# Seven staging tiles instead of four for the weight loads of an expert layer, in a pool that closes before the next layer's pool opens

## The chip, the core and the metric

The kernel runs on one core of a Trainium2 chip. The core has a matrix engine (TensorE, "PE" in the rows, with its weight loads as "PEld"), a vector engine (VectorE, "DVE"), a scalar engine (ScalarE, "ACT"), GpSimd ("POOL"), and SyncE ("SP"), whose queue issues most of the DMA transfers. Each engine works through its own instruction stream in program order, and an instruction that waits holds up everything behind it on that engine. The metric is the time of one execution in microseconds; lower is better.

## What is computed

The reference chains three layers over 1,536 tokens of width 512, all in float32:

```
attn = clustered attention over q, k, v     # 2 batches, 8 heads, 768 positions, 64 wide
x    = attn as [1536, 512]
# first expert layer: 8 experts, each token goes to one of them
e    = argmax(x @ w_gate)
y[t] = gate_w[t] * eom[t, e] * (relu(x[t] @ w1[e]) @ w2[e])   # w1 [8,512,1024], w2 [8,1024,512]
# second layer, dense
h    = y @ w_in                       # [512, 2048]
out  = (h * sigmoid(h)) @ w_out       # [2048, 512]
```

## The kernel before, in words

After the attention, `moe1` runs the first expert layer and `moe2` the dense second layer. The instruction order of each engine comes from the framework's scheduler, which orders the instructions by a simulated timeline; the kernel's own calls set what may run and from which buffers.

**Weights.** Each float32 weight block of 128 partitions by 1,024 numbers (512 KB) is loaded by one DMA of the SP queue into a staging tile (line 925), and then split into a high and a low part, which fill one half each of a tile `w` of the pool `wp` (16 tiles, two experts' worth). ScalarE writes the high part (line 894), and VectorE or GpSimd subtracts it from the staging tile to get the low part (line 899; with the `wn` counter every third one goes to GpSimd). The staging tile comes free when that subtraction has ended. The first twelve blocks stage in `wp` itself; from then on `stage()` takes tiles of tag `raw` from the pool `gp`, four of them. The queue holds loads in program order, so a load that waits for a staging tile also holds back the loads behind it and the reads of token rows (line 828).

**Units.** The first layer is a list of ten units: experts 1 to 5 with two blocks of 128 tokens each, one single-block unit for overflowing tokens, experts 6 and 7, and the two blocks of expert 0 as single-block units. Each unit needs eight weight blocks. A unit `expert(...)` runs eight groups of twelve matmuls (`hp`, line 1000); after each group ScalarE takes the Relu (`HH`, line 1001) and VectorE its low part (`HL`, line 1002); then come the matmuls of the second product (`yp`, line 1016, with `HH` and `HL` as stationary operands), the scaling `ys` (line 1021) and an indirect DMA of GpSimd that scatters the rows to `x2` (line 818). Between the groups the unit calls the next weight loads, eight per unit. Single-block units go through a transposed form (`hr`, `htp`, `H`, lines 981 to 988) and take one staging tile for `hr`. The labels tile `f` of a unit (lines 944 and 945) takes one of three buffers, which the scatter of an earlier unit still reads.

**Second layer.** The weights `w_in` and `w_out` arrive as 64-bit numbers, 32 loads of 512 KB ("halves" below). Each goes through two ScalarE operations and two VectorE operations on the staging tile (lines 1166 to 1171), then the same split, the low part always on GpSimd. The first four blocks (eight halves of `w_in`) are called from `moe1`, the other 24 halves from `moe2`, one block per step f of its first token block (`w2.pop(0)()`). `load2` reads the token rows back from `x2` (line 828), transposes them (`tp`, line 1201) and splits them into `XH` and `XL`. Steps f=0 to 15 then multiply by `w_in` (`hp`, line 1246), take the sigmoid (lines 1252 and 1253), split into `GH` and `GL`, and multiply by `w_out` (`op`, line 1225); `sg`, `GH` and `GL` are two tiles each in `gp`.

So `gp` holds four staging tiles of 4 KB a partition and six tiles of 2 KB, 28 KB a partition. It opens when `free()` closes the pools of the attention's rows, and lives to the end.

Of the kernel before, what the change touches and what calls it, by code (L numbers as in the profile page):

```python
# [11 lines left out]
F32 = mybir.dt.float32  # L12
# [18 lines left out]
class Att:  # L31

    def __init__(s, tc, ctx, q, k, v, cent, const, ident, xb, router=None):
        s.tc = tc
        s.nc = tc.nc
        s.q_ = q
        s.k = k
        s.v = v
        s.cent = cent
        s.xb = xb  # L40
        s.router = router
        P = lambda name, bufs, **kw: ctx.enter_context(tc.tile_pool(name=name, bufs=bufs, **kw))
        s.const = const
        s.ident = ident
        s.ld = P('att_ld', 2)
        s.ns = P('att_ns', 1)
        s.ohp = P('att_oh', 1)
        s.mkp = P('att_mk', 1)
        s.qk = P('att_qk', 2)
        s.cp = P('att_c', 1)  # L50
        s.sm = P('att_sm', 3)
        s.sm2 = P('att_sm2', 2)
        s.pp = P('att_pp', 4)
        s.p16 = P('att_p16', 3)
        s.pt = P('att_pt', 4)
        s.vp = P('att_v', 2)
        s.vq = P('att_vq', 1)
        s.ps_s = P('ps_s', 2, space=PSUM)
        s.ps_t = P('ps_t', 3, space=PSUM)
        s.ps_o = P('ps_o', 1, space=PSUM)  # L60
# [570 lines left out]
class Moe:  # L631

    def __init__(s, tc, ctx, const, ident, wg, wog, w1, w2, w_in, w_out, out, xb):
        s.sc = {}
        s.wn = 0
        s.gp = None
        s.spare = None
        s.hold0 = 1
        s.lows = []
        s.tc = tc  # L640
        s.nc = tc.nc
        s.c = const
        s.ident = ident
        s.w1 = w1
        s.w2 = w2
        s.w_in = w_in
        s.w_out = w_out
        s.out = out
        s.xb = xb
        s.wg = wg  # L650
        s.wog = wog
        dr = ctx.enter_context(tc.tile_pool(name='dram', bufs=1, space=bass.MemoryType.DRAM))
        s.xo = dr.tile([NCH * 128, RW], F32, name='xo')
        s.xst = dr.tile([E * CAP, RW], F32, name='xst')
        s.x2 = dr.tile([2 * NT * 128, DM], F32, name='x2')
# [253 lines left out]
    def stage(s):  # L909

        if s.gp:
            return s.gp.tile([128, 1024], F32, tag='raw', name='stage', bufs=4)
        if s.spare is None:
            t = s.wp.tile([128, 2, 1024], F32, tag='w', name='stage2')
            s.spare = t[:, 1]
            return t[:, 0]
        t = s.spare
        s.spare = None
        return t
# [347 lines left out]
def build(tc, q, k, v, centroids, moe_w_gate, moe_w_output_gate, moe_w1, moe_w2, moe2_w_in, moe2_w_out, out):  # L1267
    nc = tc.nc
    with ExitStack() as ctx:
        const = ctx.enter_context(tc.tile_pool(name='const', bufs=1))  # L1270
        ident = const.tile([128, 128], F32, name='ident')
        make_identity(nc, ident)
        cx = ExitStack()
        xp = cx.enter_context(tc.tile_pool(name='xbp', bufs=1, side='right'))
        xb = [xp.tile([128, NT, RW], F32, name=f'xb{b}') for b in range(2)]
        m = Moe(tc, ctx, const, ident, moe_w_gate, moe_w_output_gate, moe_w1, moe_w2, moe2_w_in, moe2_w_out, out, xb)
        with ExitStack() as c3:
            m.consts(cx.enter_context(tc.tile_pool(name='route', bufs=1, side='right')))
            att = Att(tc, c3, q, k, v, centroids, const, ident, xb, router=m.pair)
            att.ones = m.ones  # L1280
            m.att = att
            att.bgdma = [lambda d=d, z=z: nc.sync.dma_start(d, z) for d, z in m.zeros()]
            att.after_load = m.load_router
            att.run()
        m.pools(ctx)

        def free():
            cx.close()
            return ctx.enter_context(tc.tile_pool(name='gp', bufs=2, side='right', reuse_waits='tile'))
        X, w2 = m.moe1(m.weights2(), free)  # L1290
        with tc.high_priority():
            m.chunks = nc.values_load(m.tot[0:1, 0:1], min_val=1, max_val=NCH, skip_runtime_bounds_check_because='chunk count is bounded by the token count')
        m.moe2(m.gp, X, w2)
        m.rest()
# [18 lines left out]
```

## Time and profile before

| what | value |
|---|---|
| median of 3 runs | 793.61 us (791.09 to 793.64) |
| profiled execution, its own time | 794.19 us |
| span of the trace in that execution | 792.5 us |
| PE busy over the span | 742.1 us, 94% |
| loads of `w1` and `w2` | 72 of 512 KB each |
| loads of `w_in` and `w_out` | 32 of 512 KB each |

The profiled execution is 0.58 us above the median; 1.7 us of it lie outside the span. Times in rows are microseconds from the span's start. The first expert layer runs from about 280 to 497 us, the second layer from there to the end; attention comes before.

### The profile page before, as it was taken

To read this page: it belongs to the slowest core of one execution; us is meant where nothing else is said; L and a number is where in the kernel's file an instruction comes from. 1 tells how busy PE (TensorE), PEld (TensorE's weight loads), DVE (VectorE), ACT (ScalarE), POOL (GpSimd) and SP (SyncE) were. 2 spreads that over 40 slices of the span, in tenths; PEclk is the share of its full clock that TensorE was granted. 3 is DMA by queue.
4 is the path that set the end of the run, shared out by engine and by line. 5 is a ranking of instruction groups with operands and counts; after the bars stand their busy time and mean duration, and the time that the engine had idled before them with its cause. 6 is when DMAs were issued, how large, how long until landed. Compare 5 with 4: busy or idle time off the path is not lost.

```text
span 792.5 us, 14080 instructions
## 1 busy us (share of the span) xinstructions
PE 742.1 (94%) x5498; PEld 625.6 (79%) x5498; DVE 467.7 (59%) x830; ACT 433.7 (55%) x703; POOL 318.1 (40%) x259
## 2 busy tenths in 40 slices
PE   7889999999997799999999999799999999999996
PEld 6788998999887478888978877587687888878885
DVE  6769887977785565555557683789524222232222
ACT  5769889988764435654556663788423222122222
POOL 5677878788631365443334552445300000000000
PEclk8779999999988899999999999999999999999999
DMA  8879998998993377876658735756101000010001
GB/s 270 173 151 215 200 181 176 188 195 179 196 171 121 137 259 229 296 268 230 205 159 285 261 116 191 242 166 207 34 1 53 1 1 0 1 54 0 1 1 55
DMA packets 132983, 116.30 MB, mean 147 GB/s; under 512 B 97607, under 2 KB 103751, under 8 KB 132912
## 3 DMA queue, kind: packets, MB, share of 16 engines
q1 hardware_dynamic: 129632, 109.03, 52.0%
q0 software_dynamic: 3280, 6.33, 2.1%
q8 instruction: 44, 0.72, 0.4%
q14 instruction: 27, 0.22, 0.1%
HBM read 71.67 MB, written 18.45 MB: 114 GB/s over the span
## 4 chain that ended last, share of the span: by engine, by line
PE 53%; DVE 14%; issue 11%; DMA 10%; ACT 6%; POOL 5%; POOLq 0%; ACTq 0%; DVEq 0%; SPq 0%
PE op L1225 14%; PE hp L1246 13%; DMA stage<-in_moe_w 4%; PE yp L1016 4%; PE sp L398 3%; PE hp L1000 3%; POOL w L899 3%; PE sp L400 3%; DVE m L419 3%; DMA x<-ys,f 3%; DVE pt L456 2%; PE tp L190 2%; ACT p L421 2%; PE ptp L445 2%; DMA stage<-in_moe_w_out 2%
## 5 line engine op out<-in xcount | busy, mean ns | idle before, releaser
L899 POOL TENSOR_TENSOR w<-stage,w 128x512 fp32r<-128x512 f32 (+1 forms) x54 | 101.3, 1880 | 120.5 <-ACT w L894 113.8
L1246 PE MATMUL hp<-XH,w 128*128 128x512 f32 (+1 forms) x392 | 124.3, 394 | 3.9 <-DVE sg L1253 3.1
L894 ACT ACTIVATE w<-stage 128x1024 fp32r<-128x1024 f32 (+1 forms) x104 | 96.6, 942 | 55.0 <-DMA stage<-in_moe_w 30.2
L419 DVE TENSOR_REDUCE m<-sp 128x1 f32<-128x768 f32 x96 | 91.2, 952 | 38.8 <-PE sp L400 34.0
L1225 PE MATMUL op<-w,GH 128*128 128x512 f32 x384 | 113.2, 397 | 0.0
L465 POOL TENSOR_TENSOR p<-p,p 128x768 f16<-128x768 f32 x58 | 95.2, 1650 | 38.3 <-DVE p L464 27.8
L1253 DVE TENSOR_TENSOR sg<-hp,sg 128x512 f32<-128x512 f32 (+1 forms) x49 | 33.3, 679 | 118.2 <-ACT sg L1252 118.2
L421 ACT ACTIVATE p<-sp,m 128x768 f32<-128x768 f32 x96 | 86.3, 899 | 16.1 <-DVE m L419 15.4
L1000 PEld LDWEIGHTS hp<-X,w 128*128 128x128 f32 x672 | 86.1, 188 | 11.0 <-DVE HL L1002 5.8
L1000 PE MATMUL hp<-X,w 128*128 128x256 f32 x672 | 89.8, 283 | 4.0 <-DVE HL L1002 3.1
L1252 ACT ACTIVATE sg<-hp 128x512 f32<-128x512 f32 (+1 forms) x49 | 28.8, 589 | 116.8 <-PE hp L1246 115.8
L1246 PEld LDWEIGHTS hp<-XH,w 128*128 128x128 f32 x392 | 73.2, 188 | 23.0 <-DVE sg L1253 4.8
L1225 PEld LDWEIGHTS op<-w,GH 128*128 128x128 f32 x384 | 71.9, 188 | 17.5 <-ACT GH L894 0.7
L899 DVE TENSOR_TENSOR w<-stage,w 128x1024 fp32r<-128x1024 f32 x50 | 67.9, 1371 | 28.9 <-ACT w L894 27.3
L1246 PE MATMUL hp<-XL,w 128*128 128x512 f32 (+1 forms) x196 | 75.1, 391 | 1.6 <-DVE XL L899 1.6
L1225 PE MATMUL op<-w,GL 128*128 128x512 f32 x192 | 68.3, 397 | 1.3 <-DVE GL L899 1.3
L1016 PE MATMUL yp<-w,HH 128*128 128x512 f32 x224 | 63.7, 401 | 3.0 <-ACT HH L1001 2.7
L489 PE MATMUL o<-vh,pt 128*128 128x66 f16 x576 | 64.6, 198 | 0.4 <-DVE pt L456 0.4
L491 PE MATMUL o<-vh,pt 128*128 128x66 f16 x576 | 63.5, 195 | 1.5 <-issue 1.5
L398 PE MATMUL sp<-KA,QA 128*128 128x384 f32 x192 | 61.0, 400 | 3.2 <-ACT p L421 2.7
L490 PE MATMUL o<-vl,pt 128*128 128x64 f16 x576 | 63.9, 194 | 0.2 <-issue 0.2
L489 PEld LDWEIGHTS <-pt 128*128 128x128 f16 x576 | 53.6, 99 | 9.7 <-issue 8.6
(216 smaller groups left out, 1432.3 us busy)
## 6 DMA issues: line engine op xcount, KB each, us to landing
stage<-in_moe_w SPq DMA_DIRECT2D x72, 512.0 KB
stage<-in_moe_w_in SPq DMA_DIRECT2D x16, 512.0 KB
stage<-in_moe_w_out SPq DMA_DIRECT2D x16, 512.0 KB
xst<-z SPq DMA_DIRECT2D x8, 516.0 KB
xt<-xst SPq DMA_DIRECT2D x6, 516.0 KB
vt<-in_v SPq DMA_DIRECT2D x4, 768.0 KB
xt<-x SPq DMA_DIRECT2D x6, 512.0 KB
out_x<-os SPq DMA_DIRECT2D x12, 256.0 KB
```

What stands on the lines that cost most here:

```text
L398: nc.tensor.matmul(sp[:, g, :384], lhsT=QA[:, t], rhs=KAf[:, g * 384:(g + 1) * 384], start=True, stop=False)
L419: st['min'] = nc.vector.tensor_reduce(m, sv, axis=AX.XY, op=ALU.min).ins
L421: st['exp'] = nc.scalar.activation(p32, sv, AF.Exp, bias=m, scale=-1.0).ins
L465: s.nc.gpsimd.tensor_sub(p16[:, 1], p32, p16[:, 0])
L489: nc.tensor.matmul(o[:, t, 0:D + 2], lhsT=pt[:, 0, kt], rhs=vh[:, kt], start=kt == 0, stop=False)
L490: nc.tensor.matmul(o[:, t, 0:D], lhsT=pt[:, 0, kt], rhs=vl[:, kt], start=False, stop=False)
L894: s.nc.scalar.activation(hi, src, AF.Copy)
L899: f = lambda: (eng or s.nc.vector).tensor_sub(lo, src, hi).ins
L1000: nc.tensor.matmul(hp, lhsT=W1[k][w][:, f * 128:(f + 1) * 128], rhs=x[:, k, :N], start=n == 0, stop=n == 11)
L1016: nc.tensor.matmul(yp, lhsT=h[:, f, i * 128:(i + 1) * 128], rhs=w, start=n == 0, stop=n == 23)
L1225: nc.tensor.matmul(op[i], lhsT=g[:, i * 128:(i + 1) * 128], rhs=w, start=f == 0 and m == 0, stop=f == 15 and m == 2)
L1246: nc.tensor.matmul(h, lhsT=I[k, f // 8][w][:, fs], rhs=x[:, k, c], start=n == 0, stop=n == 11)
```

## The change

Two staging pools take the place of one. `free()` now opens a pool `wst` that holds only staging tiles, seven of them (28 KB a partition, what `gp` took as a whole). It is closed after `moe1` has been written out, and `gp` with its four staging tiles and its six tiles for the second layer is opened on the same space; a tile of `gp` then waits until the tiles of `wst` under it have been released.

```diff
@@ -634,6 +634,7 @@
         s.gp = None
+        s.raws = 7
         s.spare = None
@@ -909,7 +910,7 @@
         if s.gp:
-            return s.gp.tile([128, 1024], F32, tag='raw', name='stage', bufs=4)
+            return s.gp.tile([128, 1024], F32, tag='raw', name='stage', bufs=s.raws)
@@ -1286,8 +1287,12 @@
         def free():
             cx.close()
-            return ctx.enter_context(tc.tile_pool(name='gp', bufs=2, side='right', reuse_waits='tile'))
+            return cy.enter_context(tc.tile_pool(name='wst', bufs=2, side='right', reuse_waits='tile'))
+        cy = ExitStack()
         X, w2 = m.moe1(m.weights2(), free)
+        cy.close()
+        m.raws = 4
+        m.gp = ctx.enter_context(tc.tile_pool(name='gp', bufs=2, side='right', reuse_waits='tile'))
```

The scheduler then orders some instructions anew (lines of the changed kernel are one higher from 637 on). Three places matter below.

On the SP queue, at the end of the first layer (`w_in` and `w_out` are loads of second-layer halves, `xt_7251` and `xt_7267` are the first reads of `x2`). Before:

```order
L925 DMA stage<-in_moe_w 128x1024 x4
L925 DMA stage<-in_moe_w 128x2x512 x4
L1161 DMA stage<-in_moe_w_in 128x1024 x8
L1161 DMA stage<-in_moe_w_out 128x1024 x2
L828 DMA xt_7251<-x_72 128x2x512
L828 DMA xt_7267<-x_72 128x2x512
L1161 DMA stage<-in_moe_w_out 128x1024 x5
```

and in the changed kernel:

```order
L1162 DMA stage<-in_moe_w_in 128x1024 x8
L829 DMA xt_7251<-x_72 128x2x512
L829 DMA xt_7267<-x_72 128x2x512
L1162 DMA stage<-in_moe_w_out 128x1024 x6
L829 DMA xt_7770<-x_72 128x2x512
```

The first two loads of `w_out` moved behind the reads of `x2`, because their staging tiles now belong to `gp`.

On ACT, around the last single-block unit (`hr` and `H`) and the first `XH` of the second layer. Before:

```order
L984 ACTIVATE stage<-hr 128x512 x2
L1166 ACTIVATE stage<-stage 128x512
L1169 ACTIVATE stage<-stage 128x512
L894 ACTIVATE H<-htp 128x512 x2
L1166 ACTIVATE stage<-stage 128x512
L1169 ACTIVATE stage<-stage 128x512
L894 ACTIVATE w<-stage 128x512 x2
L1166 ACTIVATE stage<-stage 128x512
L1169 ACTIVATE stage<-stage 128x512
L894 ACTIVATE XH<-tp_7253 128x4x128
L894 ACTIVATE XH<-tp_7260 128x4x128
```

and in the changed kernel:

```order
L985 ACTIVATE stage<-hr 128x512 x2
L895 ACTIVATE H<-htp 128x512 x2
L895 ACTIVATE XH<-tp_7253 128x4x128
L1167 ACTIVATE stage<-stage 128x512
L1170 ACTIVATE stage<-stage 128x512
L1167 ACTIVATE stage<-stage 128x512
L1170 ACTIVATE stage<-stage 128x512
L895 ACTIVATE XH<-tp_7260 128x4x128
```

The work on the first halves of `w_out` moved from ahead of `H` to behind the first `XH`.

On DVE, in expert 3's unit (`f` is the labels tile, `w_5782` and `w_5802` are low parts of weight blocks). Before:

```order
L899 TENSOR_TENSOR w_5782<-stage,w_5782 128x1024
L944 COPY f<-xt 128x2 x2
L945 COPY f<-xt 128x2
L899 TENSOR_TENSOR w_5802<-stage,w_5802 128x1024
L1002 SCALAR_TENSOR_TENSOR HL<-hp,HH 128x256 x3
```

and in the changed kernel:

```order
L900 TENSOR_TENSOR w_5782<-stage,w_5782 128x1024
L900 TENSOR_TENSOR w_5802<-stage,w_5802 128x1024
L1003 SCALAR_TENSOR_TENSOR HL<-hp,HH 128x256 x2
L945 COPY f<-xt 128x2 x2
L946 COPY f<-xt 128x2
```

The label copies moved behind two `HL`; in the unit of expert 7 they moved behind two `HL` in the same way. On ACT a Relu `HH` moved behind one more weight split at eight places of the layer.

## Rows read from the trace of the kernel before

**Rows 1.** The page: its first line, and PE's busy time.
```profile
span 792.5 us, 14080 instructions
PE 742.1 (94%) x5498; PEld 625.6 (79%) x5498; DVE 467.7 (59%) x830; ACT 433.7 (55%) x703; POOL 318.1 (40%) x259
```
**Rows 2.** Stretches: length; busy PE, PEld, DVE, ACT, POOL; clock; DMA share; GB/s.
```profile
300.00:345.00 45.00, 43.07 (x271) 37.34 (x270) 28.13 (x39) 29.24 (x41) 23.27 (x12) 1.00 0.85 282
345.00:402.00 57.00, 55.38 (x350) 48.89 (x349) 30.43 (x49) 28.11 (x42) 19.82 (x11) 1.00 0.64 212
402.00:462.00 60.00, 56.46 (x335) 47.71 (x334) 41.21 (x58) 37.21 (x58) 27.88 (x15) 1.00 0.73 243
462.00:503.00 41.00, 37.55 (x185) 28.63 (x184) 25.27 (x32) 23.22 (x42) 16.88 (x13) 1.00 0.45 152
503.00:565.00 62.00, 57.38 (x247) 43.83 (x248) 55.34 (x65) 47.39 (x81) 31.47 (x21) 1.00 0.58 187
```
**Rows 3.** Waits, 295 to 500 us: SP queue, PE, ACT, DVE (us, times, longest).
```profile
SPq L925 <- DVE w L899: 39.5, 19, 7.5
SPq L925 <- POOL w L899: 38.1, 16, 4.9
...
PE hp L1000 <- DVE HL L1002: 3.1, 4, 1.1
PE yp L1016 <- ACT HH L1001: 2.3, 4, 0.7
...
ACT w L894 <- DMA stage<-in_moe_w: 27.1, 27, 2.0
...
DVE f L944 <- DMA x<-ys,f: 9.0, 7, 3.8
```
**Rows 4.** Timeline of PE: matmuls behind its waits in the first layer.
```profile
338.26 1.20 PE L1016 MATMUL yp<-w,HH 128*128 128x512 f32 x4 [0.68 <-ACT HH L1001]
...
346.76 1.68 PE L1000 MATMUL hp<-X,w 128*128 128x256 f32 x12 [0.78 <-DVE HL L1002]
...
364.29 1.20 PE L1016 MATMUL yp<-w,HH 128*128 128x512 f32 x4 [0.72 <-ACT HH L1001]
...
430.90 1.69 PE L1000 MATMUL hp<-X,w 128*128 128x256 f32 x12 [1.09 <-DVE HL L1002]
...
460.37 1.20 PE L1016 MATMUL yp<-w,HH 128*128 128x512 f32 x4 [0.72 <-ACT HH L1001]
...
490.43 0.73 PE L1016 MATMUL yp<-w,H 128*128 128x512 f32 x2 [0.94 <-ACT H L894]
```
**Rows 5.** Timeline of DVE: the label copies ahead of two late `HL`.
```profile
344.94 0.24 DVE L944 COPY f<-xt 128x2 int32<-128x2 int32 x2 [1.09 <-DMA x<-ys,f]
...
429.10 0.21 DVE L944 COPY f<-xt 128x1 int32<-128x1 int32 x2 [1.74 <-DMA x<-ys,f]
```
**Rows 6.** Timeline of ACT: a late load, and the last unit's `H`.
```profile
362.91 1.06 ACT L894 ACTIVATE w<-stage 128x1024 fp32r<-128x1024 f32 x1 [1.89 <-DMA stage<-in_moe_w]
...
488.68 0.68 ACT L1166 ACTIVATE stage<-stage 128x512 f32<-128x512 f32 x1
...
489.81 1.05 ACT L894 ACTIVATE H<-htp 128x512 fp32r<-128x512 f32 x2
```
**Rows 7.** Timeline of the SP queue between the two layers.
```profile
473.63 2.96 SPq L1161 DMA_DIRECT2D stage<-in_moe_w_out  x2
486.30 0.89 SPq L828 DMA_DIRECT2D xt<-x  x2
```
**Rows 8.** Waits of PE, 496 to 513 us, into the second layer.
```profile
PE hp L1246 <- DVE XL L899: 1.6, 1, 1.6
PE tp L1201 <- DVE XL L899: 1.1, 2, 0.5
```
**Rows 9.** Line 1246 alone: stretch, its length, PE busy (matmuls), PEld.
```profile
502.90:553.80 50.90, 27.22 (x105) 19.48 (x106) 1.00 0.65 208
```
**Rows 10.** Line 899 alone: stretch, its length, DVE busy (count), POOL busy (count).
```profile
485.00:543.25 58.25, 11.58 (x15) 23.87 (x16) 1.00 0.62 209
```

## The prediction

> **What bounds the kernel now.** I began with the page. PE is busy 742.1 of 792.5 us [rows 1], so at most 50.4 us of the span are PE's idle time, and what lies in the attention is out of the change's reach. Next I read the stretches from 300 us on [rows 2]: PE is not busy for 45.00 - 43.07 = 1.93 us, then 1.62, 3.54, 3.45 and 4.62 us, together 15.2 us. The clock is 1.00 throughout, so no part of the forecast comes from the clock. These 15.2 us are the most that better staging could give back, if no engine's work were shortened (the change shortens none). The third view is that of the waits [rows 3]. The longest wait is the SP queue's: loads of line 925 waited 39.5 us for VectorE's low part and 38.1 us for GpSimd's, that is, for a staging tile to come free. This is the resource that the change widens. But SP is not the engine that counts. What reaches PE is far smaller: its second product waited 2.3 us for `HH`, and its first 3.1 us for `HL`, four times each. Between the two lies ScalarE, which waited 27.1 us in 27 waits for a load before it could write a high part. A late load holds ScalarE, and behind it in program order stands a Relu that PE wants.
>
> So the profile shows a chain with a large loss at its start (77.6 us of the queue) and a small one at its end (5.4 us of PE). I price the end.
>
> **The change part by part.**
>
> *Three more staging tiles.* A load of 0.524 MB at the 282 GB/s of the busiest stretch [rows 2] takes 0.524 / 0.282 = 1.86 us, so three more tiles let the queue run 3 x 1.86 = 5.6 us further ahead. ScalarE's longest wait for a load was 2.0 us [rows 3]; with 5.6 us more lead such waits should go wherever the DMA engines have room. They have it from 345 us on (share 0.64 and 0.73) and hardly from 300 to 345 us (0.85) [rows 2]. What PE gets back are the waits for `HH`: the one at 364.29 us was 0.72 us [rows 4], and ScalarE shows why, since just ahead of it a high part waited 1.89 us for its load [rows 6]. The one at 338.26 us was 0.68 us [rows 4]. Of the 2.3 us, 0.72 at 460.37 us belong to the next paragraph but one; I take the other 2.3 - 0.72 = 1.6 us as given back. From below it is nothing, if loads come no earlier.
>
> *The label copies.* At 344.94 us VectorE waited 1.09 us, and at 429.10 us 1.74 us, for a scatter to finish reading its old labels tile, ahead of an `HL` [rows 5]; PE then waited 0.78 us at 346.76 and 1.09 us at 430.90 [rows 4], together 1.87 us. The order shows both copies behind two `HL` afterwards. The copies' wait does not vanish, and what is queued behind it on VectorE is the next low part. So I take 1.4 of the 1.87 us; the bounds are 0 and 1.87.
>
> *Where the loads of the second layer begin,* around 457 us, PE waited 0.72 us for `HH` [rows 4], and of the 3.1 us for `HL` about 3.1 - 1.87 = 1.2 us lie outside the two places above. This stretch is crowded on ScalarE too (37.21 of 60.00 us [rows 2]). I take 0.5 us, with bounds of 0 and 1.9.
>
> *`H` of the last unit.* It began at 489.81 us, right behind work on `w_out` that had begun at 488.68 [rows 6], and PE waited 0.94 us for it at 490.43 [rows 4]. The new order puts `H` first. I take the whole, 0.9 us: 1.13 us of ScalarE's work leave its path, more than the wait.
>
> *Into the second layer.* PE waited 1.6 and 1.1 us for `XL` [rows 8]. `XH` moves ahead of the work on `w_out`, and `XL` follows from it. But the read of the token rows was issued at 486.30 us only [rows 7], and it needs the last scatters. I take 1.0 us, with bounds of 0 and 2.7.
>
> *New waits.* At eight places a Relu stands behind one more high part, and the first transpose of `load2` moves. Where the load is there, a high part costs ScalarE 1.06 us [rows 6], which the next group of matmuls (12 in 1.68 us [rows 4]) covers. I take 1.0 us of loss for all of it; the bounds are 0 and the second rival.
>
> *The hand-over to the second pool.* The first two loads of `w_out` were issued at 473.63 us [rows 7]. Now they stand behind the reads of `x2`, so at 486.30 + 0.89 = 487.2 us at the earliest, 13.6 us later. I cost this at nothing, because the weights are ready long before PE asks. The tightest of those that I followed is the last quarter of the second half of `w_in`: its low part is the 16th of GpSimd's since 485 us and had ended by 543.25 [rows 10], and PE wants it after 8 steps of 12 matmuls and 9 more, 105 of line 1246, at 553.8 us [rows 9]. That is 10.6 us of cover. The 13.6 us don't arrive there whole: ScalarE took up the first of these halves only at 488.68 us [rows 6], 15 us after its load was issued. With two reads and a load to move first (3 x 1.86 = 5.6 us) the half is there at about 492.8 us, some 4 us later than it was taken up before. Without that cover it costs 13.6 - 10.6 = 3.0 us.
>
> The same moment is a second hazard: the first `sg`, `GH` and `GL` can't be written until staging tiles under them have been released. The last splits of the first layer come before `H` of the last unit (489.81 us [rows 6]), the first `sg` after the first group of line 1246 (from 502.9 us [rows 9]). Its cost is nothing, with 13 us of cover.
>
> **The sum.** 1.6 + 1.4 + 0.5 + 0.9 + 1.0 - 1.0 = 4.4 us. Against the profiled execution of 794.19 us (span 792.5 and 1.7 around it) that is 789.8 us; this execution lies 0.58 us above the median of 793.61, so for a median I say **789.2 us**. The upper bound of the gain is the whole of these waits, 2.3 + 3.1 + 0.94 + 2.7 = 9.0 us, or 784.6 us. The lower bound is no gain and the new waits, 793.61 + 1.0 = 794.6 us.
>
> **A rule against the change.** PE's busy share of 94% [rows 1] against its waits of 5.4 us [rows 3] bears on it. The Trainium skill, Perfetto Trace Analysis, section "Identifying Performance Opportunities", says that a kernel is in general improved by improving the engine with the highest occupancy. By that rule this change, which leaves PE's matmuls as they are, brings next to nothing: about 793 us where the waits make it 789.2. The same section, under "Optimization Strategy", names repeated gaps on the engine that should be full as a possible sign of too few buffers, which speaks for it. Which of the two holds is a matter of the gaps' size, and here they are small; the first rival is that case.
>
> **The rivals.**
>
> *1. No change, about 792 us.* The queue waits less, and PE waits as before. For it speaks that 77.6 us of the queue's waits make only 5.4 us of PE's [rows 3]; that from 300 to 345 us the DMA engines are at 0.85 [rows 2], so that loads issued earlier only queue longer; and that part of the PE waits come from scatters and not from loads [rows 5]. Then only the reordered `H` and a little else remain: a gain of 0.5 to 3.9 us. Against it speak the ScalarE waits of 1.9 us where the DMA share is 0.64.
>
> *2. Slower, about 800 us.* Place: the eight Relus that now stand behind one more high part. If the loads are no earlier, each of these waits for its load first, by the mean 27.1 / 27 = 1.0 us [rows 3], and PE waits behind it: 8 x 1.0 = 8.0 us lost, against 0.9 + 1.0 us from `H` and `XL`: 6 us slower. It decides from the point at which the load lands no earlier before the ScalarE instruction reaches it. Against it: an order with more lead has 5.6 us to spend on a wait of 1.0.
>
> *3. The hand-over shows.* If the 13.6 us arrive whole, PE waits 3.0 us at about 554 us, the gain shrinks to 1.4 us, and the time is 792.2 us. If the halves behind it then come no faster than PE uses them, it grows beyond 4 us and the kernel is slower, near 798 us.
>
> **How the numbers follow.** A measurement of this kernel can tell about 0.5%, 4.0 us, from no change. The forecast (a gain of 4 to 9 us) gets 0.50: the order shows its steps, but its sum stands close to the bound. The first rival gets 0.34, the second 0.09, the third 0.07 (0.05 at 792.2, 0.02 slower). Faster is the forecast alone, 0.50; the same is 0.34 + 0.05 = 0.39; slower 0.09 + 0.02 = 0.11. The range of 784.6 to 794.6 us takes in the bounds of the sum, the first rival and the third's milder half, and leaves out the 0.11 and little below.
>
> **What would show it.** Right: from 345 us on ScalarE's waits for loads fall well below 27.1 us and the queue's for staging tiles below 77.6; PE's waits for `HH` and `HL` fall from 5.4 to below 3 us; the 0.94 us ahead of the last `yp` are gone; PE's idle time of 15.2 us in the five stretches falls to about 11. Wrong by rival 1: the queue's waits fall and PE's don't. By rival 2: a Relu that stands right behind a high part that waited, with a PE wait behind it, at several places. By rival 3: a wait of line 1246 or 1225 for `w` between 520 and 600 us. What would make it wrong altogether is a moved instruction on VectorE or GpSimd that these rows don't price.

## The result: 0.5% slower

The changed kernel takes 796.88 us in the median of 20 executions, and the kernel before, run beside it, 792.99 us. The ratio is 1.0053, with a 95% interval of 1.0034 to 1.0072: slower, by 4.2 us of 793 (the two medians differ by 3.9). The forecast was 789.2 us.

The profiled execution of the changed kernel has a span of 794.7 us. Its first row and its five stretches answer to [rows 1, 2]; a line number of the changed kernel is one higher than in the kernel before.

```profile
span 794.7 us, 14080 instructions
PE 742.7 (93%) x5498; PEld 627.3 (79%) x5498; DVE 477.3 (60%) x830; ACT 431.8 (54%) x703; POOL 320.1 (40%) x259
```

Stretches of the changed kernel (length; busy PE, PEld, DVE, ACT, POOL; granted clock; DMA share; GB/s):

```profile
300.00:345.00 45.00, 41.97 (x265) 36.71 (x264) 35.90 (x41) 28.29 (x40) 24.32 (x12) 1.00 0.93 329
345.00:402.00 57.00, 53.04 (x339) 47.04 (x338) 31.31 (x46) 25.29 (x39) 18.27 (x10) 1.00 0.60 191
402.00:462.00 60.00, 54.80 (x318) 46.80 (x317) 46.46 (x60) 39.37 (x61) 29.23 (x14) 0.97 0.68 230
462.00:503.00 41.00, 40.11 (x206) 32.01 (x205) 17.40 (x24) 17.44 (x33) 13.87 (x12) 1.00 0.30 108
503.00:565.00 62.00, 56.17 (x241) 42.20 (x239) 52.99 (x65) 48.63 (x84) 31.07 (x22) 1.00 0.63 207
```

PE is not busy for 3.03, 3.96, 5.20, 0.89 and 5.83 us. Up to 462 us that is 12.19 us, where the kernel before has 7.09; from 462 to 503 us it is 2.56 us less than before; behind it 1.21 us more. So the change gives back what the forecast expected between the layers and loses twice as much inside the first one. VectorE is busy for 7.8 us more in the first stretch, with only two instructions more.

Comparing whole spans understates this. The first matmul of the first expert layer begins at 278.40 us in this execution and at 280.39 in that of the kernel before, with the same instructions ahead of it; in all the executions shown below it begins between 273.0 and 282.0 us. From there to the end of the span it is 794.7 - 278.40 = 516.3 us after, and 792.5 - 280.39 = 512.1 before: 4.2 us more, as the ratio says. This length is used below beside the ratios.

The waits from 295 to 500 us answer to [rows 3] (us, times, longest); the last two rows are of the SP queue:

```profile
PE hp L1001 <- DVE HL L1003: 9.3, 7, 1.9
...
DVE f L945 <- DMA x<-ys,f: 4.2, 1, 4.2
...
ACT w L895 <- DMA stage<-in_moe_w: 2.0, 2, 1.2
...
PE yp L1017 <- DVE HL L1003: 0.8, 1, 0.8
...
SPq L926 <- DVE w L900: 38.5, 17, 5.5
SPq L926 <- POOL w L900: 26.2, 11, 5.3
```

The loads now come early: ScalarE waits 2.0 us for them, where it waited 27.1, and no second product waits for `HH` any more, where it was 2.3 us. But PE's waits for `HL` have trebled, from 3.1 to 9.3 us. The next two rows show why, the low parts of weight blocks from 295 to 500 us by engine (count, busy us, mean ns, then idle time ahead):

```profile
L900 DVE TENSOR_TENSOR w<-stage,w 128x1024 fp32r<-128x1024 f32 x41 | 69.7, 1712 | 15.8 <-ACT w L895 15.6 <-issue 0.2
L900 POOL TENSOR_TENSOR w<-stage,w 128x1024 fp32r<-128x1024 f32 x22 | 56.3, 2559 | 67.9 <-ACT w L895 66.4 <-PE htp L988 1.3
```

The same 41 low parts of VectorE took 57.2 us in the kernel before, 1404 ns each:

```profile
L899 DVE TENSOR_TENSOR w<-stage,w 128x1024 fp32r<-128x1024 f32 x41 | 57.2, 1404 | 27.2 <-ACT w L894 25.8 <-POOL w L899 1.4
```

One place shows what a long one is. In the timelines of GpSimd, VectorE and PE of the changed kernel (start, duration):

```profile
335.38 2.39 POOL L900 TENSOR_TENSOR w<-stage,w 128x1024 fp32r<-128x1024 f32 x1
...
335.57 3.28 DVE L900 TENSOR_TENSOR w<-stage,w 128x1024 fp32r<-128x1024 f32 x1
338.78 0.74 DVE L1003 SCALAR_TENSOR_TENSOR HL<-hp,HH 128x256 fp32r<-128x256 f32 x2
339.44 1.21 DVE L900 TENSOR_TENSOR w<-stage,w 128x1024 fp32r<-128x1024 f32 x1
...
339.24 1.68 PE L1001 MATMUL hp<-X,w 128*128 128x256 f32 x12 [1.25 <-DVE HL L1003]
```

GpSimd's low part runs to 335.38 + 2.39 = 337.77 us. VectorE's, begun 0.2 us behind it, ends at 335.57 + 3.28 = 338.85, that is 1.08 us after GpSimd's has ended. Alone, at 339.44, the same instruction takes 1.21 us. So nearly all of VectorE's work (1.08 of 1.21 us) came after GpSimd had ended, and the profile counts the time before it as busy. `HL` stood behind it, and PE waited 1.25 us. The next one has the same sum:

```profile
356.36 2.72 POOL L900 TENSOR_TENSOR w<-stage,w 128x1024 fp32r<-128x1024 f32 x1 [0.61 <-ACT w L895]
...
357.09 3.07 DVE L900 TENSOR_TENSOR w<-stage,w 128x1024 fp32r<-128x1024 f32 x1
```

GpSimd ends at 356.36 + 2.72 = 359.08, VectorE at 357.09 + 3.07 = 360.16, which is 1.08 us later. Every low part of VectorE from 295 to 500 us that took longer than 1.3 us (14 in the changed kernel, 8 in the kernel before) began while one of GpSimd was running, and ended 1.08 to 1.09 us after it. In the kernel before, 4 of the 41 low parts of VectorE overlap one of GpSimd by half of their length or more; in the changed kernel it is 14.

The Trainium skill, "SBUF — State Buffer", section "SBUF: two separate sides", states such a rule: VectorE and GpSimd share a pair of ports; between an instruction of VectorE with two SBUF inputs and one of GpSimd that reads SBUF, the one that starts first has the pair for the whole instruction, and the other blocks. The trace agrees, with these 1.08 us behind the end.

### The profile page after: what moved, and what is told of

Read it like the earlier page. It is cut to its first block, busy times and chain, and to the rows that moved or that the text cites. A ratio compares the mean times of both kernels' runs of the same rounds, so it can differ in the third digit from the quotient of the medians.

```text
span 794.7 us, 14080 instructions
## 1 busy us (share of the span) xinstructions
PE 742.7 (93%) x5498; PEld 627.3 (79%) x5498; DVE 477.3 (60%) x830; ACT 431.8 (54%) x703; POOL 320.1 (40%) x259
## 5 line engine op out<-in xcount | busy, mean ns | idle before, releaser
L900 POOL TENSOR_TENSOR w<-stage,w 128x512 fp32r<-128x512 f32 (+1 forms) x54 | 103.1, 1913 | 122.2 <-ACT w L895 104.3
L895 ACT ACTIVATE w<-stage 128x1024 fp32r<-128x1024 f32 (+1 forms) x104 | 94.5, 940 | 28.5 <-DVE stage L1172 12.1
L900 DVE TENSOR_TENSOR w<-stage,w 128x1024 fp32r<-128x1024 f32 x50 | 80.4, 1623 | 17.8 <-ACT w L895 17.6
```

The source lines that it names most:

```text
L895: s.nc.scalar.activation(hi, src, AF.Copy)
L900: f = lambda: (eng or s.nc.vector).tensor_sub(lo, src, hi).ins
```

## The experiments

**Theory A**: seven tiles bring the loads early, ScalarE then writes high parts one right behind the other, and the low parts that follow fall into the same time on both engines; VectorE's are held up, and `HL` behind them is late. **Theory B**: the new order puts more low parts ahead of `HL`, whatever their length. **Theory C**: the hand-over between the pools costs. A was formed from the trace above. Each ratio is to the kernel before, timed beside the experiment.

| kernel | ratio (95% interval) | VectorE's low parts: count, mean ns | PE's `hp` waits for `HL`, us | first matmul to end, us |
|---|---|---|---|---|
| before | | 41, 1404 | 3.1 | 512.1 |
| changed: seven tiles | 1.0053 (1.0034 to 1.0072) | 41, 1712 | 9.3 | 516.3 |
| four tiles, two pools | 0.9967 (0.9936 to 0.9997) | 41, 1394 | 1.5 | 512.2 |
| five tiles | 1.0001 (0.9970 to 1.0031) | 41, 1666 | 6.8 | 512.2 |
| seven, none on GpSimd | 0.9978 (0.9949 to 1.0008) | 62, 1220 | 5.9 | 510.3 |
| before, none on GpSimd | 1.0006 (0.9977 to 1.0035) | 62, 1220 | 2.0 | 512.6 |
| before, every 2nd on GpSimd | 1.0026 (0.9990 to 1.0063) | 31, 1808 | 2.0 | 517.2 |
| seven, every 6th on GpSimd | 0.9955 (0.9925 to 0.9985) | 51, 1379 | 6.3 | 510.3 |
| five, none on GpSimd | 0.9971 (0.9943 to 0.9999) | 63, 1220 | 1.4 | 512.6 |
| seven, GpSimd in halves | 0.9973 (0.9952 to 0.9994) | 41, 1485 | 5.2 | 510.9 |

Only the ratios compare executions on the same chip. The last three columns come from one profiled execution of each kernel, on different chips, and counts and waits are from 295 to 500 us. In five rows a fall of the granted clock to about 0.5 is part of the last column: changed (456 to 460 us), five, none on GpSimd (280 to 284 and 464 to 472), GpSimd in halves (449 to 453), before, every 2nd (360 to 365) and before, none on GpSimd (502 to 507). By an estimate from PE's busy time and the clock there, worked out for the first of them further below, each costs 1.6 to 1.7 us, and the two of the five tiles 4.5 us together. So a difference of 1 or 2 us in this column shows nothing without the ratio beside it.

**The hand-over alone, and five tiles.**

```diff
-        s.raws = 7
+        s.raws = 4
```

> The changed kernel with four staging tiles in the first pool instead of seven: the hand-over between the two pools alone. Theory A (seven tiles bring the loads early, so the low parts of GpSimd and VectorE run at the same time, VectorE's takes about 2.7 us instead of 1.21, and an HL behind it is late): without the extra tiles the low parts are as before (mean near 1.40 us), PE waits for HL about 3 us and not 9.3, and the time is that of before or up to 2.5 us less (ratio 0.997 to 1.000). Theory C (the hand-over of the space costs): PE loses as much as with seven tiles, ratio 1.004 to 1.006.

> The changed kernel with five staging tiles in the first pool. Theory A: ScalarE's wait for loads falls from 27.1 us part of the way, the low parts of VectorE lie between 1.40 and 1.71 us in the mean, the time between before and the changed kernel (ratio 0.998 to 1.004). Theory C: as with seven, 1.004 to 1.006.

With four tiles and two pools the kernel is 0.3% faster than before, not slower: C falls as the cause. Where the 0.3% come from is open: the profiled execution shows no gain from the first matmul to the end (512.2 against 512.1 us). Five tiles lie between the two, as A has it: the low parts are nearly as long as with seven, and ScalarE's waits for loads have fallen to 6.1 us.

**The overlap taken away.**

```diff
-        return s.nc.gpsimd if s.wn % 3 == 0 and s.wn > 8 else s.nc.vector
+        return s.nc.vector
```

> Seven tiles, but in the first layer VectorE computes every low part and GpSimd none (41 + 22 on VectorE). Theory A: no low part of VectorE is longer than 1.3 us there, PE's waits for HL fall from 9.3 to below 4 us, and the time falls below the changed kernel's by 4 us or more, to that of before or less (ratio 0.994 to 1.000). Theory B (HL is late because the new order puts more low parts ahead of it, whatever their length): 22 low parts more stand on VectorE, PE's waits for HL grow beyond 9.3 us, ratio 1.006 or more.

> The kernel before, with every low part of the first layer on VectorE. Theory A: only four of its low parts overlapped GpSimd's, so there is little to win: ratio 0.997 to 1.002, and a smaller gain than the same edit brings with seven tiles. Theory B: 22 low parts more ahead of HL, ratio 1.003 or more, as much as with seven tiles.

VectorE now has 62 low parts and not 41, and every one takes 1.22 us, so that all of them together need hardly more time (73.8 us) than 41 did with GpSimd's help (69.7 us). With seven tiles, the low parts and PE's waits for `HL`:

```profile
L900 DVE TENSOR_TENSOR w<-stage,w 128x1024 fp32r<-128x1024 f32 x62 | 73.8, 1220 | 15.5 <-ACT w L895 15.0
...
PE hp L1001 <- DVE HL L1003: 5.9, 6, 1.4
```

The stretch from 300 to 400 us in the same kernel, and then in the kernel before:

```profile
300.00:400.00 100.00, 98.62 (x620) 87.21 (x619) 69.47 (x101) 55.02 (x81) 8.22 (x8) 1.00 0.76 258
```

```profile
300.00:400.00 100.00, 96.45 (x606) 84.42 (x605) 58.56 (x87) 55.52 (x80) 42.39 (x22) 1.00 0.74 243
```

PE is busy 98.62 of 100 us, against 96.45 in the kernel before (and 96.67 in that kernel with none on GpSimd). This is what early loads are worth when nothing takes it back. Up to 400 us PE waits 0.9 us for `HL`, against 5.8 us up to 405 us in the changed kernel. The other 5.0 us of the 5.9 come at 440 to 456 us, where work on `w_in` joins the low parts and VectorE is full:

```profile
436.00:456.00 20.00, 14.75 (x88) 11.61 (x87) 18.26 (x29) 14.25 (x26) 6.62 (x4) 1.00 0.62 202
```

The time falls by 6 us against the changed kernel's ratio, as A expects; the waits for `HL` (5.9 us, below 4 expected) fall less than it expects. B expected more than 9.3 us and a slower kernel, and falls. The same edit to the kernel before brings nothing (1.0006): there was little overlap to take away.

**More and less of it.** In the kernel before, every second block on GpSimd (`% 2`); with seven tiles, every sixth (`% 6`); with five tiles, none.

> The kernel before with four staging tiles, every second instead of every third weight block's low part on GpSimd: the suspected cost without any extra tile. Theory A (what hurts is that both engines compute low parts at the same time): more than the 4 of 41 low parts of before overlap GpSimd's by over half, VectorE's mean rises above 1.40 us although it has fewer of them, and the kernel is slower, ratio 1.002 to 1.008. Theory B (number of low parts that the order puts ahead of HL): VectorE has 31 and not 41 of them, so HL is earlier, ratio 1.000 or less.

> Seven tiles, every sixth weight block's low part on GpSimd instead of every third. Theory A: about half of the 14 overlapped low parts stay, VectorE's mean lies between 1.22 and 1.71 us, PE's waits for HL between 5.9 and 9.3 us, and the time between the two kernels with seven tiles (ratio 0.998 to 1.005 to before). Theory B: more low parts on VectorE than with every third, PE's waits for HL above 9.3 us, slower than the changed kernel.

> Five tiles in the first pool, no low part on GpSimd in the first layer. Theory A: without overlap more tiles can only help, so at or below the five-tile kernel with GpSimd (1.000) and the hand-over alone (0.997): ratio 0.994 to 0.998. Theory B: HL late behind 22 more low parts, ratio above 1.000.

Every second block on GpSimd makes VectorE's low parts longer than in the changed kernel (1808 ns) without any extra tile. The ratio is not clear, 1.0026 with an interval that holds 1. The way to PE is another than A said, as the waits of this kernel show:

```profile
PE yp L1016 <- ACT HH L1001: 4.1, 7, 1.3
PE hp L1000 <- DVE HL L1002: 2.0, 4, 1.0
```

With four tiles the long low parts give staging tiles back late, ScalarE waits 35.4 us for loads (27.1 before), and `HH` is late, not `HL`. But these waits for `HH` and `HL` together are only 0.7 us longer than in the kernel before (6.1 against 5.4), so most of the 5.1 us by which the last column is longer stays unexplained. Every sixth block on GpSimd does better than A's number: only 4 low parts overlap by half or more, not 7, and the ratio is 0.9955. Five tiles without GpSimd fit by their ratio (0.9971).

**The overlap made shorter.** GpSimd's low part in two instructions:

```diff
-            f = lambda: (eng or s.nc.vector).tensor_sub(lo, src, hi).ins
+            f = lambda: [(eng or s.nc.vector).tensor_sub(lo[:, c], src[:, c], hi[:, c]).ins for c in
+                ((slice(0, 512), slice(512, 1024)) if eng is s.nc.gpsimd and lo.shape[-1] == 1024 else (slice(None),))][-1]
```

> Seven tiles; GpSimd computes each low part of the first layer in two instructions of 512 columns instead of one of 1024. Theory A, in the form the traces give it (a low part of VectorE that begins during one of GpSimd's starts its own 1.1 us only when that instruction has ended): VectorE now waits for at most half as long, its overlapped low parts fall from 2.69 to about 1.9 us, PE's waits for HL fall from 9.3 to 4 to 7 us, and the time falls by 2 to 4 us against the changed kernel (ratio 0.999 to 1.003 to before). Theory B (the number of low parts ahead of HL): the same number is ahead, PE waits about 9 us, ratio 1.004 to 1.007.

VectorE's low parts, and PE's waits for `HL`:

```profile
L900 DVE TENSOR_TENSOR w<-stage,w 128x1024 fp32r<-128x1024 f32 x41 | 60.4, 1485 | 16.4 <-ACT w L895 16.1 <-issue 0.2
...
PE hp L1001 <- DVE HL L1003: 5.2, 6, 2.1
```

GpSimd still does every third block, VectorE still 41, and now VectorE waits for half an instruction. Its mean falls from 1712 to 1485 ns, PE's waits for `HL` to 5.2 us, and the ratio to 0.9973, below the 0.999 expected. This is the run that B can explain least, because no block changes its engine. The granted clock fell here as in the changed kernel, and the time from the first matmul to the end is 5.4 us shorter all the same, so that fall alone is not what made the changed kernel slower. GpSimd pays: 15 of its halves begin during a low part of VectorE, end 1.14 to 1.17 us behind it, and take 2.0 to 2.3 us where 1.3 is usual.

**A fourth label tile, and addresses.** I thought that the waits for `HL` that remain without GpSimd might come from label copies.

```diff
-        s.fp = P('fp', 3)
+        s.fp = P('fp', 4)
```

> Seven tiles, no low part on GpSimd in the first layer, and four label tiles instead of three, so that a label copy need not wait for a scatter. If the remaining PE waits for HL (5.9 us, most of them at 440 to 456 us) come from the label copies: VectorE's waits for scatters (9.0 us, 3 times) go, PE's waits for HL fall to about 3 us, and the time is 2 us less than without the fourth label tile (ratio 0.994 to 0.997). If they come from VectorE being full there (stage work of the second layer beside the low parts): no change, ratio 0.997 to 0.999.

The ratio is 0.9877 (0.9843 to 0.9910), from 7 executions, and the first matmul to the end takes 507.0 us. PE's waits for `HL` fell to 3.7 us (5.9 without the fourth tile), near the expected 3. But the label copies still wait 7.7 us for scatters (9.0), so the reason is not the expected one. And the 507.0 us account for only 5.1 of the 9.8 us that the ratio stands for; the rest is open (the profiled execution was the slowest of the seven). Matmuls of the first layer followed each other faster. A label tile is 32 bytes a partition, so a fourth one moves the pools behind it (`X`, `XH`, `XL`, `HH`, `HL`, `H` and `ys`) from 32 bytes beside a multiple of 64 onto one. Padding the label tile does the same with three tiles and leaves every instruction in its place:

```diff
-        f = s.fp.tile([128, 2, 4], F32, tag='f', name='f')
+        f = s.fp.tile([128, 4, 4], F32, tag='f', name='f')
```

> The kernel before with the label tile padded from 32 to 64 bytes a partition: the same instructions in the same order, but the pools behind it (XH, XL, HH, HL) begin at multiples of 64 bytes and not 32 bytes beside. If the run with the fourth label tile was fast for the moved addresses (its second-product matmuls followed each other every 229 ns and not 234): 229 ns here too, the time from the first matmul of the layer to the end falls from 512.1 to about 509 us, ratio 0.993 to 0.997. If it was fast for the fourth label tile itself: 234 ns, ratio 0.998 to 1.002.

> The changed kernel with the label tile padded to 64 bytes, nothing else. Against the kernel before with the same padding, run beside it, the change should lose again what it lost without it, 4 us (ratio to that run 1.003 to 1.007), if its cause is the overlap and not the addresses that it moved.

> Seven tiles, every sixth block on GpSimd, the label tile padded to 64 bytes: the two gains together. If they add: 0.9955 from the first and 3 us from the second, ratio 0.990 to 0.994. If the addresses do nothing, 0.994 to 0.998.

The kernel before, padded, has a ratio of 0.9965 (0.9938 to 0.9992), and from the first matmul to the end it takes 783.8 - 273.9 = 509.9 us, 2.2 less than unpadded. The 72 matmuls of `hr` from 295 to 500 us took 395 ns each in the kernel before and after; padded:

```profile
L981 PE MATMUL hr<-w,X 128*128 128x512 f32 x72 | 17.2, 390 | 0.0
```

The changed kernel, padded, has 1.0007 (0.9985 to 1.0029): 789.09 / 785.71 = 1.0043 times the kernel before, padded, timed on the same chip; each of its 12 executions (787.32 us and more) lies above that kernel's median. So the change loses nearly the same again, 3.4 us, with other addresses. Every sixth block on GpSimd with seven padded tiles has 0.9927 (0.9897 to 0.9958): the two gains add, 0.9955 x 0.9965 = 0.9920, which the interval holds. It and the kernel with the fourth label tile beat both kernels of this case.

## Why the prediction was wrong, step by step

**Three more staging tiles** (1.6 us of gain): right in its own terms. PE's waits for `HH` are gone, and ScalarE's for loads fell to 2.0 us.

**The label copies** (1.4 us of gain): their waits fell from 9.0 to 4.2 us, but the gain that I put to them was PE's wait for `HL`, and that grew by 6.2 us. The copies were one cause of late `HL` and not the one that grows.

**Where the loads of the second layer begin** (0.5 us of gain): wrong. At 448 to 456 us PE waits 1.59 and 1.92 us for `HL`, behind low parts and work on `w_in`. This is a second cause, beside the overlap of low parts. Up to 436 us PE's `hp` waits 5.8 us for `HL` (2.6 before), and 0.9, 3.5 and 2.2 us with seven tiles and none, every sixth block or halves on GpSimd. From 436 to 462 us it waits 3.5 us (0.5 before), and in those three runs still 4.9, 2.8 and 3.0. VectorE is busy for all of 452 to 462 us, against 8.29 of these 10 us in the kernel before. An instruction of VectorE on `w_in` that takes 0.68 us in the median takes 2.95 us at 450.44, beside a low part of GpSimd that runs from 450.42 us for 2.42 us. Then the granted clock falls, as these stretches of the changed kernel show. The prediction had given the clock no term, because it read 1.00 in every stretch of the kernel before.

```profile
448.00:450.00 2.00, 0.98 (x5) 0.45 (x3) 2.00 (x3) 2.00 (x5) 1.33 (x1) 1.00 0.94 338
450.00:452.00 2.00, 1.43 (x12) 1.43 (x13) 2.00 (x3) 2.00 (x5) 1.98 (x2) 1.00 0.95 262
452.00:454.00 2.00, 1.67 (x9) 1.04 (x7) 2.00 (x3) 0.93 (x3) 1.83 (x2) 1.00 0.89 309
454.00:456.00 2.00, 0.42 (x3) 0.42 (x4) 2.00 (x4) 1.07 (x2) 0.26 (x1) 1.00 0.92 352
456.00:458.00 2.00, 2.00 (x12) 1.93 (x11) 2.00 (x5) 0.16 (x1) 0.00 (x0) 0.62 0.16 62
458.00:460.00 2.00, 2.00 (x6) 1.58 (x5) 2.00 (x5) 2.00 (x5) 0.00 (x0) 0.52 0.00 0
```

PE was busy for 4.50 us from 448 to 456 us; then the clock was near its lower level (1.2 of 2.4 GHz) for most of 4 us, which costs an estimated 2.00 x 0.38 + 2.00 x 0.48 = 1.7 us. The padded changed kernel has the same order and about the same waits for `HL` (9.9 us), no such drop, and is 1.9 us longer than the padded kernel before from the first matmul to the end. How often the clock drops in executions that were not profiled is open, and so is how the 4.2 us divide between waits and clock.

**`H` of the last unit** (0.9) and **into the second layer** (1.0): right, and a little small. The wait of 0.94 us ahead of the last `yp` is gone, and of 1.6 and 1.1 us for `XL` [rows 8] one of 1.0 is left.

**New waits** (1.0 us of loss): this is the step that failed. I priced only ScalarE's instructions, a Relu behind one more high part. The new wait was on VectorE. In place of 1.0 us of loss the runs showed 6.2 us more of PE's waits for `HL` (9.3 and not 3.1). The first 3.2 us of them, up to 436 us, are those that shrank where the overlap was taken away or shortened; the other 3.0 stand where work on `w_in` fills VectorE. I named the next low part as what is queued behind a label copy, but left only 1.87 - 1.4 = 0.47 us for it, and took a low part's duration as fixed. The kernel before already shows that it isn't: its mean is 1404 ns, and the one that begins at 339.44 us in the changed kernel takes 1.21 us alone. The last sentence of the prediction names this way of being wrong, an instruction on VectorE that its rows don't price.

**The hand-over** (nothing): nearly right. With four tiles and two pools the kernel is not slower, and no wait of PE for `w`, as the third rival has it, stands in the second layer of the changed kernel. But from 503 to 620 us PE waits 3.4 us for `sg` (2.1 before; 3.3 with four tiles and two pools), 1.3 us that I had not counted.

**The rivals.** The second had the right sign and the wrong engine: it put a high part that waits for its load ahead of a Relu. Loads were early, and no Relu made PE wait. The first (no change) is off too, since PE's waits did not stay as they were. That the queue waits less was also wrong: with the rows that name `HL` as releaser (29.6 us before, which I had left out, and 42.3 after) it waited 107.2 us before and 107.0 after. The queue fills every tile that there is, and then waits as long.

## What to carry to other kernels

Earlier data moves the work that waited for it, and work that was apart in time may then fall together. Before giving a stream more buffers, list the instructions behind each landing on every engine, and look in the trace for two of them that take longer side by side than alone: compare the shortest with the mean of one shape. Time that an engine spends blocked inside an instruction shows as busy, so no view of waits names it.

## What was not expected of the hardware

With tiles that begin at a multiple of 64 bytes PE was faster than with tiles 32 bytes beside one, with the same instructions in the same order: a matmul of `hr` took 390 and not 395 ns, though of its operands only the stationary one (`X`) had moved. From the first matmul to the end the kernel before was 2.2 us shorter, of which 0.8 us are shorter waits for `HH` (1.5 and not 2.3 us); seven tiles with every sixth block on GpSimd were 3.0 us shorter (507.3 and not 510.3). Why is not shown. 62 low parts on VectorE alone took 73.8 us, hardly more than 41 beside GpSimd's 22 (69.7 us): with seven tiles, GpSimd's help was worth 4.1 us of VectorE's time.
